# A low-rank step one loop step later, its lines drained by two engines, and zero products issued as pairs of row halves

## The chip, the cores and the metric

The kernel runs on one core of a Trainium2 chip. The time is that of the whole launch on the device, in microseconds (us). The core's engines are TensorE (PE in the profile; PEld are its weight loads), VectorE (DVE), ScalarE (ACT), GpSimd (POOL) and SyncE (SP); each runs its own instructions in order and they meet through semaphores.

## The reference

The input x is 8 batches of 3136 rows and 256 columns, float32. It is first mixed by Fourier transforms, then by a low-rank step over the rows and an MLP over the columns:

```python
X = np.fft.fft(np.fft.fft(x, axis=1), axis=2)
x = X.real
h = x.transpose(0, 2, 1) @ U @ V            # U: 3136 x 32, V: 32 x 3136
u = x + h.transpose(0, 2, 1)
out = u + np.maximum(u @ w_ch1, 0) @ w_ch2  # w_ch1: 256 x 1024, w_ch2: 1024 x 256
```

## The kernel before

The row transform of length 3136 is split as 49 times 64, with the symmetry of real input used so that only 25 of the 49 residues (NK1) are kept. Batches go in four pairs. For every batch there is a table g: for each of the 25 residues 128 rows, of which 64 hold a half-transformed batch and 64 hold the low-rank result te, the same for all 25. One product with the table T then gives both the second half of the transform and the low-rank term; the results go into a tile q, and the MLP reads q.

The front builds the tables (sine values, T, the folded weights) and the g of batch 0. x of batch 0 comes by DMA as the tile X0. x_round issues the products of X0 with the table Fs (quarter_products, line 227; 128 in the first round, 128 in the second), and the results are copied out of PSUM into zt, by copy_act or copy_dve, and from there into g by quarter_rows. line32 (line 204) makes one further row with four products. Ahead of the first round and behind the second PE runs products of zeros (the tile idle, which is a part of W1m) into the PSUM tile that comes next (lines 650 and 674); nobody reads their results. w1_fold (line 679) folds the MLP's first weights. te_single (line 298) computes the low-rank result of one batch from g with 50 products, te_out lets DVE copy it to te, and spread lets POOL write te into the 64 lower rows of g (line 306).

The loop goes over 13 chunks for each pair, with four loop steps each, so 52 steps for each pair (NS). In loop step t of a chunk, mlp1 (line 383, ReLU on ACT in line 385) runs for that chunk, mlp2 (lines 394 and 397) for the chunk before, then what plan has placed at that step, then the outputs are drained (om on ACT in line 406, ob on DVE in lines 407 and 408) and stored by SP (line 412). plan writes the order out by hand: place(steps, lo, hi) spreads a list of steps evenly over the loop steps lo to hi.

For pair 0 the plan holds, among others: turned_steps, which makes the g of batch 1 in loop steps 10 to 17 (products line 227, zt on ACT, eight copies into g on DVE each second step, line 76); te_single of batch 1; the s3_steps of batch 1, twelve groups of four residues and a last one (line 322), each drained from PSUM into q by the engine that is given to it; and the steps of the next pair: loads of x (xa by SP, xb by an indirect DMA of POOL, line 99), folds on POOL (line 144) and DVE (lines 134 to 136), and s1_steps (line 185, drained into z by ACT, line 73). The steps of s1, s3 and te_single share one pool of two PSUM tiles (psd); mlp1 has two of its own (psh), mlp2 has two (pso).

copy_dve is line 76, copy_act line 73. copy_alt calls the two by turns.

Of the kernel before, what the change touches and what calls it, by code (L numbers as in the profile page):

```python
# [22 lines left out]
def kernel(  # L23
# [9 lines left out]
    nc = tc.nc  # L33
# [3 lines left out]
    P = 128  # L37
# [124 lines left out]
    def load_steps(pr):  # L162

        for c in range(8):
            def load(c=c):
                pr.chunks.append(load_pair_chunk(pr.p, c))
            yield load, (lambda c=c: fold_pair_chunk(pr.chunks[c])), (lambda c=c: fold_pair_chunk_d(pr.chunks[c]))
# [92 lines left out]
    def turn(pr, b, parts, engines=(nc.sync,)):  # L260
        g = gpool.tile([P, NK1, D], BF16, tag=f"g{b}", name="g")
        src = zd[pr.p % 2, b].rearrange("k cn d -> cn k d")
        for i, (k0, k1) in enumerate(parts):
            engines[i % len(engines)].dma_start(out=g[0:64, k0:k1], in_=src[:, k0:k1, :])
        pr.g[b] = g

    def te_out(pr, b, ps, c0, s0, spread):
        te = tes[b]
        nc.vector.tensor_copy(te[64:96, 0:129], ps[c0:c0 + 32, 0, 0:129])
        nc.vector.tensor_copy(te[96:128, 129:256], ps[s0:s0 + 32, 0, 129:256])  # L270
        spread(pr.g[b], te)

    def te_steps(pr, spread):

        st = Obj()
        order = [*range(1, 32), 0]

        def step(lo, hi):
            if lo == 0:
                st.ps = psd.tile([P, 2, D], FP32, tag="ps", name="teps")  # L280
            for i in range(lo, hi):
                j = order[i]
                for s, cs in enumerate([slice(0, 129), slice(129, 256)]):
                    nc.tensor.matmul(st.ps[64 * s:64 * s + 64, 0, cs], UZ[:, j, s::2],  # L284
                                     pr.z[:, j, cs], start=(i == 0), stop=(i == 31))
            if hi == 32:
                for b in range(2):
                    te_out(pr, b, st.ps, 32 * b, 64 + 32 * b, spread)

        for lo, hi in [(0, 20), (20, 32)]:  # L290
            yield lambda lo=lo, hi=hi: step(lo, hi)

    def te_single(pr, b, spread, ps=None):

        ps = ps or psd.tile([P, 2, D], FP32, tag="ps", name="teps")
        for k in range(NK1):
            for s, cs in enumerate([slice(0, 129), slice(129, 256)]):
                nc.tensor.matmul(ps[32 * s:32 * s + 32, 0, cs], us[:, k, s::2], pr.g[b][0:64, k, cs],
                                 start=(k == 0), stop=(k == NK1 - 1))
        te_out(pr, b, ps, 0, 32, spread)  # L300

    def spread(parts):
        def run(g, te):
            src = te[64:128].bitcast(I32)
            for eng, k0, k1 in parts:
                eng.tensor_copy(g[64:128, k0:k1].bitcast(I32), src.unsqueeze(1).to_broadcast([64, k1 - k0, D // 2]))  # L306
        return run

    def two(row, a, b, n):

        v = row[:, a:a + n]
        return bass.AP(row.tensor, v.offset, [list(v.ap[0]), [b - a, 2], [1, n]])

    def s3_steps(pr, b, evac):

        if pr.q is None:
            pr.q = qpool[pr.p % 2].tile([P, 2, 6272], BF16, tag="q", name="q")

        def mm(o, k1, blk, st, rows=P, low=None):
            lt = low[:, blk::2] if low is not None else pr.g[b][0:rows, k1, blk::2]  # L320
            r = T[0:rows, k1, 0:64] if k1 == 0 else T[0:rows, k1, :].rearrange("p (s j) -> p s j", s=2)
            nc.tensor.matmul(o, lt, r, start=st, stop=True, skip_group_check=True)  # L322

        def lines(ps, g, blk, rows, low=None):
            for u in range(4):
                us = slice(u * 64, (u + 1) * 64)
                mm(ps[:, 0, us] if 4 * g + u == 0 else ps[:, :, us], 4 * g + u, blk, u == 0 and low is None, rows, low)

        def step(g, blk):
            ps = psd.tile([P, 2, 256], FP32, tag="ps", name="ps")  # L330
            lines(ps, g, blk, P)
            move(ps, g, blk, evac)

        def move_part(ps, g, blk, evac, part):
            lo = 64 if part and g == 0 else 0
            c0 = 3200 + b * 1536 + (4 * g - 1) * 64 if part else b * 1600 + 4 * g * 64
            evac(pr.q[:, blk, c0 + lo:c0 + 256], ps[:, part, lo:256])

        def move(ps, g, blk, evac):
            if g == 0:  # L340
                move_part(ps, g, blk, evac, 0)
                move_part(ps, g, blk, evac, 1)
            else:
                k0 = 4 * g
                evac(two(pr.q[:, blk, :], b * 1600 + k0 * 64, 3200 + b * 1536 + (k0 - 1) * 64, 256), ps[:])

        def last():
            ps = psd.tile([P, 2, 2, 64], FP32, tag="ps", name="ps")
            k1 = NK1 - 1
            for blk in range(2):  # L350
                mm(ps[:, blk], k1, blk, blk == 0)
            for blk in range(2):
                evac(two(pr.q[:, blk, :], b * 1600 + k1 * 64, 3200 + b * 1536 + (k1 - 1) * 64, 64), ps[:, blk])

        yield lines, move_part
        for g in range(6):
            for blk in range(2):
                yield lambda g=g, blk=blk: step(g, blk)
        yield last
# [124 lines left out]
    def bank2(name):  # L484
        return psh.tile([P, 2, 512], FP32, tag="h", name=name)
# [7 lines left out]
    def round_view(ps):  # L493
        return ps.rearrange("p a (i s c k) -> p (a i) s c k", s=2, c=2, k=32)
# [5 lines left out]
    idle = W1m[0][:].rearrange("p a j -> p (a j)")[:, 0:640]  # L500
# [138 lines left out]
    def x_round(ps, i0, n):  # L639
        quarter_products(X0, ps, i0, n)  # L640

        def out(evac):
            j = i0 % 16
            evac(zts[i0 // 16][:, :, :, :, j:j + n].rearrange("p c k s i -> p s c k i"),
                 ps[:, :, :, :, 0:NK1].rearrange("p i s c k -> p s c k i"))
        return out

    tps0 = bank2("tps")
    for i in range(4):
        nc.tensor.matmul(tps0[:, 0], idle[:, 0:P], idle[:, P:640], start=True, stop=True)  # L650
    x_round(round_view(tps0), 0, 8)(copy_act)
    outs = [x_round(round_view(bank_d("tps")), 8 + 4 * i, 4) for i in range(2)]
    z32 = line32(0, bank_o("ps32"))
# [16 lines left out]
    nc.vector.tensor_copy(T[0:64, :, 64:128], T[0:64, :, 63::-1])  # L670

    teps = bank2("teps")
    for i in range(5):
        nc.tensor.matmul(teps[:, 0], idle[:, 0:P], idle[:, P:640], start=True, stop=True)

    def w1_fold(c, banks):
        for blk in range(2):
# [63 lines left out]
    spread_pool = spread([(nc.gpsimd, 0, 9), (nc.gpsimd, 9, 17), (nc.gpsimd, 17, NK1)])  # L741
# [38 lines left out]
    def plan(p):  # L780

        at = [[] for _ in range(NS)]

        def place(steps, lo, hi):
            steps = list(steps)
            for i, s in enumerate(steps):
                at[lo + i * (hi - lo) // len(steps)].append(s)

        def place_next(nx, a, gap, s3lo):

            s1 = list(s1_steps(nx, copy_act))
            for c, (load, fn, fd) in enumerate(load_steps(nx)):
                for o, f in [(0, load), (4, fn), (7, fd), (9, s1[2 * c]), (10, s1[2 * c + 1])]:
                    at[int(a + gap * c) + o].append(f)
            e = int(a + gap * 7) + 11
            place([lambda: (turn(nx, 0, [(0, 8), (8, NK1)]), turn(nx, 1, whole))], e, e + 1)
            place(te_steps(nx, spread_pool), e, e + 2)
            place(list(s3_steps(nx, 0, copy_dve))[1:], s3lo, NS)

        cur = pairs[p]  # L800
        if p == 0:
            rest = []
            for t, f in zip([1, 2, 2, 3, 4, 5, 5, 6, 8], s3b0[4:]):
                at[t].append(f)
            at[0].append(lambda: w2_fold(0))
            at[2].append(lambda: w2_fold(1))
            place([late_tables], 8, 9)
            place([load_uz], 24, 25)
            place([lambda: rest.append(pair_tables())], 6, 7)
            place([lambda: rest[0]()], 10, 11)  # L810
            place(turned_steps(cur, 1, X1), 10, 18)
            place([lambda: te_single(cur, 1, spread_pool)], 18, 19)
            place(list(s3_steps(cur, 1, copy_dve))[1:], 19, 31)
            place_next(pairs[1], 8, 2.6, 44)
        else:
            place(list(s3_steps(cur, 1, copy_dve))[1:], 3, 18)
            if p + 1 < NP:
                place_next(pairs[p + 1], 0, 3.4, 40)
        return at

    for i in range(len(chunks) + 1):
        cur = chunks[i] if i < len(chunks) else None
# [47 lines left out]
```

## Time and profile before

| | |
|---|---|
| median of 5 runs | 452.45 us (451.33 to 455.52) |
| profiled execution | 451.86 us, its span 450.1 us |
| PE busy | 425.7 us, 95% of the span |
| ACT busy | 289.8 us, 64% |
| DVE busy | 225.0 us, 50% |
| POOL busy | 143.0 us, 32% |
| moved by DMA | 64.34 MB, mean 143 GB/s |

All times below are microseconds from the start of the span of the one profiled execution. A group's line names the source line, the engine, the operation, what is written and read, and how often. "x119" counts recorded instructions; some records of matmuls can be missing. A PE time includes the way through the array, so the ends of successive products overlap. In brackets stands the idle time of the engine ahead of the group and what ended it; "issue" means that the profile shows no wait for it.

### The profile page before, as it was taken

How to read it: one execution, taken by the hardware profiler on the slowest of the kernel's cores; microseconds unless marked ns; L12 is line 12 of the kernel's file. 1: busy time of each engine (PE TensorE's matmuls, PEld its weight loads, DVE VectorE, ACT ScalarE, POOL GpSimd, SP SyncE). 2: the span in 40 equal slices, each digit the busy share in tenths (PEclk: the TensorE clock that was granted, in tenths of full speed). 3: DMA queues.
4: the chain of work that ended last, by engine and by line, in shares of the span. 5: the costliest groups of instructions: out<-in, count | busy, mean ns of one | idle time of the engine just before them, and what ended most of it. 6: DMA issues, size and time to landing. Idle time of an engine off the chain costs nothing.

```text
span 450.1 us, 10536 instructions
## 1 busy us (share of the span) xinstructions
PE 425.7 (95%) x4158; PEld 308.0 (68%) x4221; DVE 225.0 (50%) x541; ACT 289.8 (64%) x402; POOL 143.0 (32%) x180
## 2 busy tenths in 40 slices
PE   3789997999999998999999999999999999999995
PEld 1656665777777776767867777776867777667764
DVE  7783686874355367362354367463354344222222
ACT  5786755767565666777565667777466655666662
POOL 7465465941420546350510545550400000000000
PEclk9999999999999999999999999999999999999999
DMA  8649763876683656763772647863662222222323
GB/s 145 160 141 168 205 169 111 254 181 179 171 212 74 170 147 194 234 209 88 161 209 63 170 112 241 225 194 106 162 144 66 71 64 67 72 71 74 80 60 93
DMA packets 59761, 64.34 MB, mean 143 GB/s; under 512 B 12950, under 2 KB 52672, under 8 KB 59552
## 3 DMA queue, kind: packets, MB, share of 16 engines
q1 hardware_dynamic: 50000, 42.68, 36.7%
q0 software_dynamic: 7232, 14.30, 13.5%
q10 hardware_dynamic: 2480, 6.69, 4.0%
q8 instruction: 33, 0.54, 0.5%
q14 instruction: 16, 0.13, 0.1%
HBM read 34.62 MB, written 32.19 MB: 148 GB/s over the span
## 4 chain that ended last, share of the span: by engine, by line
PE 80%; DVE 6%; DMA 5%; issue 3%; SPq 2%; POOL 2%; ACT 1%; DVEq 0%; POOLq 0%
PE ops L394 33%; PE hps L383 32%; PE ps L322 5%; PE ops L397 4%; DMA out_dram<-ob 2%; PE ps L185 2%; DMA X<-in_x_dram 2%; DVE g L76 2%; SPq L412 2%; PE teps L284 1%; PE tps L227 1%; DMA xa<-in_x_dram 1%; DVE q L76 1%; POOL y L144 1%; ACT hT L385 1%
## 5 line engine op out<-in xcount | busy, mean ns | idle before, releaser
L385 ACT ACTIVATE hT<-hps 128x1024 bf16<-128x1024 f32 (+1 forms) x208 | 202.5, 975 | 109.8 <-PE hps L383 103.1
L394 PE MATMUL ops<-W,hT 128*128 128x256 bf16 x1568 | 224.7, 273 | 0.8 <-DVE ob L408 0.6
L394 PEld LDWEIGHTS <-hT 128*128 128x128 bf16 x1568 | 145.1, 98 | 34.9 <-DVE ob L408 0.8
L76 DVE CAST q<-ps 128x512 bf16<-128x512 f32 (+3 forms) x121 | 65.0, 559 | 83.3 <-PE ps L322 81.9
L383 PE MATMUL hps<-q,W1p 128*128 128x512 bf16 (+1 forms) x420 | 103.2, 355 | 2.3 <-DVE q L76 0.5
L407 DVE TENSOR_TENSOR ob<-ops,om 128x256 f32<-128x256 f32 (+1 forms) x102 | 41.8, 409 | 117.7 <-ACT om L406 117.0
L383 PE MATMUL hps<-q,W1m 128*128 128x512 bf16 x351 | 95.7, 379 | 2.1 <-ACT hT L385 0.5
L144 POOL TENSOR_TENSOR y<-xa,xb 98x510 f32<-98x510 f32 (+1 forms) x48 | 61.2, 1295 | 107.3 <-DMA xa<-in_x_dram 102.2
L383 PEld LDWEIGHTS <-W1p 128*128 128x128 bf16 x448 | 40.3, 97 | 26.9 <-issue 1.7
L383 PEld LDWEIGHTS <-W1m 128*128 128x128 bf16 x384 | 35.3, 98 | 26.5 <-issue 1.4
L397 PEld LDWEIGHTS <-q 128*128 128x128 bf16 x392 | 38.4, 98 | 21.2 <-issue 0.6
L406 ACT COPY om<-ops 128x256 f32<-128x256 f32 (+1 forms) x102 | 37.3, 365 | 13.9 <-PE ops L394 7.9
L306 POOL COPY g<-te 64x1024 int32<-64x1024 int32 (+1 forms) x23 | 24.8, 1119 | 57.1 <-DVE te L270 52.5
L408 DVE TENSOR_TENSOR ob<-ops,om 128x256 f32<-128x256 f32 (+1 forms) x102 | 41.0, 402 | 0.0
L73 ACT CAST z<-ps 128x512 bf16<-128x512 f32 x48 | 28.1, 586 | 18.5 <-PE ps L185 18.5
L397 PE MATMUL ops<-Bp,q 128*128 128x128 f16 x200 | 38.4, 219 | 0.0
L322 PE MATMUL ps<-T,g 128*128 128x128 bf16 (+3 forms) x400 | 36.9, 218 | 0.4 <-ACT q L73 0.3
L397 PE MATMUL ops<-Bm,q 128*128 128x128 f16 x192 | 36.9, 219 | 0.0
L322 PEld LDWEIGHTS <-g 128*128 128x128 bf16 (+1 forms) x400 | 29.4, 98 | 5.0 <-POOL g L306 0.4
L99 POOL DMA_INDIRECT xb<-in_x_dram,idx x24 | 24.6, 1023 | 5.4 <-issue 4.5
L135 DVE TENSOR_TENSOR yb<-y 98x508 bf16<-98x508 f32 (+1 forms) x24 | 21.8, 906 | 0.0
L185 PE MATMUL ps<-yb,F 98*128 98x258 bf16 (+1 forms) x108 | 18.9, 265 | 1.7 <-DVE q L76 1.7
(136 smaller groups left out, 205.0 us busy)
## 6 DMA issues: line engine op xcount, KB each, us to landing
out_dram<-ob SPq DMA_DIRECT2D x389, 64.0 KB
xa<-in_x_dram SPq DMA_DIRECT2D x24, 392.0 KB
zturn<-z ACTq DMA_DIRECT2D x9, 512.0 KB
g<-zturn SPq DMA_DIRECT2D x3, 800.0 KB
g<-zturn SPq DMA_DIRECT2D x3, 544.0 KB
X<-in_x_dram POOLq DMA_DIRECT2D x4, 384.0 KB, 7.9
X<-in_x_dram POOLq DMA_DIRECT2D x2, 744.0 KB, 8.0
zturn<-z ACTq DMA_DIRECT2D x3, 448.0 KB
```

Source lines behind the costliest of these rows:

```text
L73: nc.scalar.copy(o, i)
L76: nc.vector.tensor_copy(o, i)
L144: nc.gpsimd.tensor_tensor(ck.y[:, l0:l1, 1:256], ck.xa[:, l0:l1, 1:256], rb[:, l0:l1, 255:0:-1], op=AL.add)
L185: nc.tensor.matmul(o[..., cs], F[:, 2 * t + i].rearrange("p b k c -> p (b k c)"), y[..., cs], start=first, stop=True, skip_group_check=True)
L322: nc.tensor.matmul(o, lt, r, start=st, stop=True, skip_group_check=True)
L383: nc.tensor.matmul(ps[:, i, 0:n], (W1p if ch.sg > 0 else W1m)[jp // 2][:, blk, j], q[:, blk, c0:c0 + n], start=(blk == 0), stop=(blk == 1))
L385: nc.scalar.activation(ch.h[:, 2 * jp:2 * jp + 2, 0:n], ps[:, :, 0:n], AF.Relu)
L394: nc.tensor.matmul(ps, ch.h[:, j, t * P:(t + 1) * P], W2[:, j, :], start=(j == 0 and (t % 2 == 0 or last)), stop=(j == JT - 1), skip_group ...
L397: nc.tensor.matmul(ps[:, j], q[:, j, tk], (Bp if ch.sg > 0 else Bm)[:, j], start=False, stop=False, skip_group_check=True)
L406: nc.scalar.copy(om[:, 0:n], ch.po[:, 0:n, 1])
L407: nc.vector.tensor_tensor(ob[:, 0:n, 0:P], ch.po[:, 0:n, 0], om[:, 0:n], op=AL.add)
L408: nc.vector.tensor_tensor(ob[:, 0:n, P:D], ch.po[:, 0:n, 0], om[:, 0:n], op=AL.subtract)
```

## The change

Two things are changed. In the front, the zero products are issued by a helper, halves, as pairs: each product takes 64 of the 128 rows, the two of a pair write the two banks of the PSUM tile, and their widths are 512 or 256 columns. The four products ahead of the first round become 14, the five behind the second round become 14. In the loop plan of pair 0, te_single of batch 1 is placed in loop step 19 instead of 18, and the s3_steps of batch 1 in 20 to 30 instead of 19 to 30, with copy_alt in the place of copy_dve.

```diff
+    def halves(ps, sizes):
+        for n in sizes:
+            for r in range(2):
+                w = idle[64 * r:64 * r + 64]
+                nc.tensor.matmul(ps[:, r, 0:n], w[:, 0:P], w[:, P:P + n], start=True, stop=True)
+
     tps0 = bank2("tps")
-    for i in range(4):
-        nc.tensor.matmul(tps0[:, 0], idle[:, 0:P], idle[:, P:640], start=True, stop=True)
+    halves(tps0, [512] * 2 + [256] * 5)
     x_round(round_view(tps0), 0, 8)(copy_act)
...
     teps = bank2("teps")
-    for i in range(5):
-        nc.tensor.matmul(teps[:, 0], idle[:, 0:P], idle[:, P:640], start=True, stop=True)
+    halves(teps, [512] * 3 + [256] * 4)
...
             place(turned_steps(cur, 1, X1), 10, 18)
-            place([lambda: te_single(cur, 1, spread_pool)], 18, 19)
-            place(list(s3_steps(cur, 1, copy_dve))[1:], 19, 31)
+            place([lambda: te_single(cur, 1, spread_pool)], 19, 20)
+            place(list(s3_steps(cur, 1, copy_alt))[1:], 20, 31)
             place_next(pairs[1], 8, 2.6, 44)
```

## The prediction

> **What bounds the kernel now.** I read the page first: the span is 450.1 us, and the profiled execution took 451.86 us with what lies around it. TensorE (PE) carries 80% of the chain that ended last, and the granted clock is full throughout.
>
> ```profile
> PE 80%; DVE 6%; DMA 5%; issue 3%; SPq 2%; POOL 2%; ACT 1%; DVEq 0%; POOLq 0%
> q8 instruction: 33, 0.54, 0.5%
> ```
>
> So only PE's stalls are for sale. The second line counts for the front: queue q8 carries 0.54 MB in 33 reads, and PE has 4158 + 4221 recorded instructions; that makes 16 kB and some 255 instructions a read, so these are PE's own instructions, in blocks. The waits of PE then show where it stood:
>
> ```profile
> PE ps L185 <- DVE q L76: 1.7, 2, 1.1
> PE teps L298 <- DVE g L76: 1.7, 2, 1.5
> PE tps L227 <- issue: 1.1, 1, 1.1
> ```
>
> The two places of the change, in the timeline. First the loop (start, length, engine, line, what; in brackets the idle time before, and who ended it):
>
> ```profile
> 68.14 3.04 DVE L76 COPY g<-zt 32x400 bf16<-32x400 bf16 x8 [0.90 <-ACT zt L73]
> ...
> 71.23 1.59 PE L298 MATMUL teps<-g,us 64*32 64x129 bf16 x50 [1.48 <-DVE g L76]
> ...
> 73.97 3.12 POOL L306 COPY g<-te 64x1152 int32<-64x1152 int32 x3 [4.60 <-issue]
> ...
> 75.17 0.57 PE L322 MATMUL ps<-T,g 128*128 128x64 bf16 x8 [0.17 <-POOL g L306]
> 75.58 1.28 DVE L76 CAST q<-ps 128x256 bf16<-128x256 f32 x4 [1.73 <-PE ps L322]
> ...
> 76.33 0.39 PE L185 MATMUL ps<-yb,F 98*128 98x258 bf16 x2 [0.59 <-DVE q L76]
> ```
>
> PE reaches the low-rank step while DVE still writes g and stands 1.48 us. It stands 0.17 us until POOL has spread the result. Then it issues two line products, and the next product L185 wants their PSUM buffer while DVE drains four pieces in a row: 0.59 us. That is 2.24 us, and of 76 to 120 us hardly anything else.
>
> Now the front:
>
> ```profile
> 13.43 1.02 PE L650 MATMUL tps<-W1m 128*128 128x512 bf16 x3 [0.35 <-ACT us L73]
> 15.07 2.16 PE L227 MATMUL tps<-Fs,X 98*32 98x50 f16 x128 [0.61 <-DMA X<-in_x_dram]
> ...
> 18.71 2.03 PE L227 MATMUL tps<-Fs,X 98*32 98x100 f16 x119 [1.14 <-issue]
> ...
> 23.16 0.39 PE L679 MATMUL w1ps<-w_f,Q 128*128 128x512 f32 x1 [0.41 <-issue]
> 23.73 1.59 PE L298 MATMUL teps<-g,us 64*32 64x129 bf16 x50 [0.18 <-DVE g L76]
> ```
>
> The zero products fill the time until x lands at 15.07. Then PE stops after 9 of the 128 products of the second round, for nothing the profile names, until 18.71. From that stop to the next nameless one (23.16) it runs 119 products with their weights (238), 5 zero products (10), four weight loads and three products of L679 (7) and one semaphore instruction: 256. So both stops are PE out of instructions at a block's edge. In the DMA view q8 starts its first read between 16.0 and 16.2 us, its second between 20.8 and 21.0. What those stops cost is told by ACT:
>
> ```profile
> 18.57 0.86 ACT L73 COPY g<-zt 31x800 bf16<-31x800 bf16 x1
> 19.81 1.62 ACT L73 CAST zt<-tps 128x800 bf16<-128x800 f32 x3 [0.38 <-PE tps L227]
> 21.46 2.21 DVE L76 COPY g<-zt 32x800 bf16<-32x800 bf16 x6 [0.56 <-ACT zt L73]
> ```
>
> ACT is in one piece until 19.43, then waits only 0.38 us for PE; DVE and the low-rank product at 23.73 hang on it. So the 1.14 us stop is worth 0.38 us, the 0.41 us one nothing (the product after it waits for DVE anyway).
>
> **The change, the loop part.** The step te_single goes from loop step 18 to 19, so PE runs one more mlp1 (0.86), mlp2 (1.0) and L185 pair (0.22) first. From the end of mlp2 at 69.75 it arrives at about 71.8; DVE's g is there at 71.2. The wait of 1.48 is gone. It ends at 73.4, DVE converts te (two times 0.29) by 74.0, POOL's first spread copy (1.15) ends at 75.2. PE meanwhile has L185, mlp1 and mlp2 (2.1) and arrives at 75.4: the 0.17 is gone by 0.2, a thin cover, and at most 0.3 comes back if POOL is late. POOL's order moves too: the xb load of chunk 4 (0.97 us of POOL) now stands ahead of the spread; POOL idled 4.60 us there, so it is free, and the fold behind the spread starts earlier. The step issues no DMA; SP's order is unchanged. On DVE the g copies and one drain of the outputs stand ahead of te as before.
>
> The drains: s3_steps now alternates. Of the pieces of pair 0, batch 1, ACT takes two of 256, five of 512 and one small one. ACT's price for a 512 piece is that of L73 z<-ps, 586 ns; so ACT gets some 4 us, DVE loses 4.5. At the first group the two engines drain side by side: the buffer is free some 0.4 us after the first product instead of 1.0, so of 0.59 about 0.2 stays. But 13 steps over 11 loop steps instead of 12 put two into loop step 25 as well, with an L185 pair behind them. That pair waits for the first drain: 0.59 to 0.69 of copy less 0.2 of the second step's products, so 0.45 new. After each of the stalls the first two products took 0.39 instead of 0.22 (76.33 against 78.63), so a stall costs 0.17 more than its idle time: three go (2.24 + 0.51), two smaller ones come (0.65 + 0.34). Sum of the loop part: -1.75 us. Bounds: -2.5 (no new stall) to -1.1 (both new ones at the full 0.59 to 0.7 and POOL late).
>
> Does it reach the end? PE is busy 23.84 of 24 us between 96 and 120. The fold of the last chunk ends at 108.98 and PE uses it from 111.24: 2.3 us of slack, enough for 1.75 even if its load does not move. Nothing else is late next.
>
> **The front part.** 4 products of 512 columns become 14 on 64 rows each, 2304 columns a row half; 5 become 14 with 2560. No row of this trace has two row halves at once. Bound below: side by side, like the column tiles of L298 (50 recorded products of 128 columns in 1.59 us, 32 ns each, against 56 ns for the single L322 of 128); then the first fill ends at 14.5, the second lasts 1.1. Bound above: one after the other, 4 x 0.215 + 10 x 0.108 = 1.95 us, to 15.4, 0.35 past the landing; the second 2.15, hidden before L679's weights. I take the lower, nearest to L298, and keep +0.35. The Trainium skill (TensorEngine Tiling: Array Packing, Key Properties) speaks against it: a change of the tiling mode drains the engine. By that rule one drain more would be paid at each fill; no run here prices it.
>
> The larger effect is the 20 instructions more ahead of x. Every block edge comes 20 instructions earlier in the work. The first read now begins about 1.1 us after PE's wait for x ends (16.16 against 15.04); the edge whose passing frees that block lies 256 back from the first stop: 18 for the nine products, 8 for L204, 230 of round one's 256. So it stands 26 instructions into round one, 28 behind the first of the two semaphore instructions of the wait for x. With the change it stands 8 behind. In the steady loop reads start, by my count, 28 to 58 instructions before PE's array reaches the freeing edge (taking the same 1.1 us of latency), and the sequencer's semaphore instructions lie 35 ahead of the array; so the fetch looks up to some 20 beyond the sequencer. 8 is inside that, 28 was not. Then the read is asked for at 13.44 instead of 15.1, arrives by about 15.5, and the stop at 18.71 goes: -0.38. The second edge then falls just before the last product of round two; its read, asked for at 16.8, is usable by about 20, and ACT wants that product at 20.6. Value taken: -0.38; bounds: -0.4 and the rival below. The Trainium skill (Runtime: NRT & Kernel Launch, Instruction fetch mechanics) gives blocks of 256 instructions, which the count above confirms, and says the refill is mostly hidden; here it was not, 1.14 us. By the rule the front part would be worth 0.
>
> **Sum.** 451.86 - 1.75 - 0.38 = 449.7 on the profiled execution's scale. The median of the runs shown is 452.45, 0.59 above it; that gives 450.3 for a median, 2.1 us or 0.47% less. The measurement can tell some 0.5% (2.3 us) from no change, so the forecast sits at that bound.
>
> **Rivals.**
> Fetch not advanced (20%): the fetch does not look 8 ahead of a blocked sequencer. Then the first stop, still until 18.7, hits the fourth product of line 32 (L204), 20 instructions earlier, and the second, still until 23.1, hits the last product of round two (2 + 254 instructions on), which ran before 20.74. ACT's last zt copy moves from about 20.95 to 23.35: +2.4, or +3.0 if the fill pairs run one after the other behind it. With the loop part: +0.65 to +1.25, 453.1 to 453.7 by the median. For it: the 8 is near; against it: the count of the steady loop.
> ACT becomes the bound (12%), the one that ends slower: in a loop step with hT 1.03, z 0.59, q 0.59 and om 0.38 ACT has 2.59 us against PE's 2.25. It decides once ACT is more than one loop step late, because hps has two buffers: then each of seven copies costs PE up to 0.59, 4.1 us, net +2, 454.5. Against it: copies fall on every second step only, and ACT was busy 13.97 of 20 us there; 18 with the copies.
> The stall moves on (6%): the loop gain is lost at the last fold or the UZ load's place on SP, the front gains nothing: 452.
>
> **How the numbers follow.** Forecast 62%: around 450.3 with 0.44 beyond the bound of 0.5% (DVE's relief and the refills are rather underpriced), 0.17 within, 0.01 slower. Fetch rival: 0.02, 0.13, 0.05. ACT: 0.01, 0.04, 0.07. Moved on: 0.01, 0.04, 0.01. Sum: faster 0.48, same 0.38, slower 0.14. Range: from -2.5 - 0.4 with 0.8 of a median's scatter (448.7) to the fetch rival's 453.7.
>
> **What would show it.** Right: no wait of L298 for g near 72 us; the second round of L227 without a nameless stop, q8's first read before 15 us, ACT's zt copies at 19.4; a PE wait of about 0.5 at L185 some 12 us after the step. Wrong: a nameless stop at L204 near 17 us and at L227 near 21; or hps waiting for hT between 76 and 100.

## The result and the profile after

The changed kernel took 453.88 us in the median of 26 runs (451.66 to 460.78), against 453.33 us for the kernel before in 47 runs (450.85 to 456.11). The ratio is 1.0006 [0.999, 1.0023]: no difference that can be told. Forecast were 450.3 us. Repeated on another chip (the last experiment) the ratio was 1.0054 [1.0024, 1.0085]. All ratios leave out executions that took over 1.5% more than the fastest of their kernel, so a ratio is not quite the ratio of the medians.

The profiled execution took 451.94 us with a span of 450.2 us, practically that of before (451.86 and 450.1). The equal spans hide a loss in the front and gains behind it; the waits of PE show where. Page, chain of work that ended last; then the waits of PE (who waited for whom, total us, times, longest):

```profile
PE 86%; DVE 4%; issue 3%; ACT 2%; DMA 2%; SPq 1%; POOL 0%; DVEq 0%; POOLq 0%
```

```profile
PE tps L227 <- issue: 2.7, 1, 2.7
PE ps L204 <- issue: 1.2, 1, 1.2
...
PE ps L185 <- DVE q L76: 0.7, 1, 0.7
PE teps L298 <- DVE g L76: 0.5, 1, 0.5
PE hps L383 <- ACT hT L385: 0.5, 2, 0.2
...
PE ps L185 <- ACT q L73: 0.5, 1, 0.5
```

The 1.5 us wait of L298 for g in the loop is gone, as forecast (the 0.5 that is left is that of batch 0, in the front). But the two nameless stops, 1.14 and 0.41 us before, are now 1.2 and 2.7 us. The front, in the timeline of PE, and below it that of ACT (start, length, what, count, in brackets the idle time before and who ended it):

```profile
13.44 1.15 PE L652 MATMUL tps<-W1m 64*128 64x512 bf16 x14 [0.30 <-ACT us L73]
14.55 2.16 PE L227 MATMUL tps<-Fs,X 98*32 98x50 f16 x128
16.49 0.33 PE L204 MATMUL ps<-x,F 98*32 98x129 bf16 x3
18.00 0.23 PE L204 MATMUL ps<-x,F 98*32 98x127 bf16 x1 [1.18 <-issue]
18.01 2.15 PE L227 MATMUL tps<-Fs,X 98*32 98x100 f16 x127
22.83 0.26 PE L227 MATMUL tps<-Fs,X 98*32 98x100 f16 x1 [2.67 <-issue]
...
25.92 1.59 PE L298 MATMUL teps<-g,us 64*32 64x129 bf16 x50 [0.52 <-DVE g L76]
```

```profile
20.30 1.22 ACT L73 CAST zt<-tps 128x800 bf16<-128x800 f32 x2
23.12 0.49 ACT L73 CAST zt<-tps 128x400 bf16<-128x400 f32 x1 [1.60 <-PE tps L227]
```

PE stops ahead of the fourth product of L204, and again 128 products later ahead of the very last product of round two. That is the rival "fetch not advanced", to the instruction: both blocks of PE's instructions end 20 instructions earlier in the work, and the next ones arrive hardly earlier than before (the stops ended at 18.71 and 23.16, and now at 18.00, with x half a microsecond earlier, and at 22.83). The second stop before cost nothing; now one product of 128 is cut off by it, ACT's last zt piece hangs on that product, and all of batch 0 on ACT. The low-rank step of batch 0 starts at 25.92 instead of 23.73.

The loop, from the step on: timelines of PE, ACT and DVE.

```profile
74.35 1.59 PE L298 MATMUL teps<-g,us 64*32 64x129 bf16 x50
...
77.99 0.57 PE L322 MATMUL ps<-T,g 128*128 128x64 bf16 x8
79.22 0.38 PE L185 MATMUL ps<-yb,F 98*128 98x258 bf16 x2 [0.66 <-DVE q L76]
...
91.53 0.38 PE L185 MATMUL ps<-yb,F 98*128 98x258 bf16 x2 [0.45 <-ACT q L73]
```

```profile
77.17 1.02 ACT L385 ACTIVATE hT<-hps 128x1024 bf16<-128x1024 f32 x1
78.40 0.65 ACT L73 CAST q<-ps 128x256 bf16<-128x256 f32 x2 [0.21 <-PE ps L322]
```

```profile
78.80 0.63 DVE L76 CAST q<-ps 128x192 bf16<-128x192 f32 x2 [0.85 <-ACT q L73]
```

No bracket ahead of L298 and L322: 1.48 and 0.17 us are gone. The 0.45 us wait at the loop step with two s3 steps, 12.3 us later, came at exactly its forecast size. The wait ahead of L185 stayed (0.66, before 0.59): the two engines do not drain side by side there. ACT begins at 78.40, as soon as a product is there; DVE begins only at 78.80, and the profile has it waiting for ACT's q (inferred by the profile; no run tests why).

To see where the two kernels stand to each other, I took three points at which PE waits for the same thing in both (the weights W1p; hT near 123 and near 425). A fourth point, a product of mlp2 near 64 us, lies between the front and the changed steps of the loop. Timeline of PE, kernel before, then the changed one:

```profile
29.51 1.02 PE L383 MATMUL hps<-q,W1p 128*128 128x512 bf16 x4 [0.44 <-DVE W1p L447]
63.22 0.27 PE L394 MATMUL ops<-W,hT 128*128 128x256 bf16 x1 [0.28 <-DVE ob L408]
122.73 1.94 PE L383 MATMUL hps<-q,W1m 128*128 128x512 bf16 x8 [0.25 <-ACT hT L385]
424.80 1.94 PE L383 MATMUL hps<-q,W1m 128*128 128x512 bf16 x8 [0.25 <-ACT hT L385]
```

```profile
31.70 1.02 PE L383 MATMUL hps<-q,W1p 128*128 128x512 bf16 x4 [0.44 <-DVE W1p L447]
65.82 0.27 PE L394 MATMUL ops<-W,hT 128*128 128x256 bf16 x1 [0.67 <-DVE ob L408]
124.24 1.02 PE L383 MATMUL hps<-q,W1m 128*128 128x512 bf16 x4 [0.25 <-ACT hT L385]
424.88 1.94 PE L383 MATMUL hps<-q,W1m 128*128 128x512 bf16 x8 [0.25 <-ACT hT L385]
```

The changed kernel is 2.19 us behind after the front, 2.60 near 64 us, 1.51 after the loop of pair 0, and 0.08 at the end. The step near 64 us is the wait for ob, which stands ahead of the changed steps and varies from profile to profile (none in e4 and e8, 0.15 to 0.79 us in the others). From there to the wait for hT near 123 us the kernel before takes 59.51 us and the changed one 58.42: the changed loop steps gain 1.09 us here, not the forecast 1.75. Of the 1.43 us between the last two points 1.09 is one stall of the kernel before at 174.4 (L185 waits for DVE's q) that this execution of the changed kernel does not have; the other 0.34 is not accounted for. The stall hangs on where POOL's fold happens to fall. Timeline of DVE and POOL, before, then after:

```profile
171.30 1.75 DVE L135 TENSOR_TENSOR yb<-y 98x508 bf16<-98x508 f32 x1
...
171.15 3.03 POOL L144 TENSOR_TENSOR y<-xa,xb 98x510 f32<-98x510 f32 x2 [4.63 <-DMA xa<-in_x_dram]
```

```profile
172.81 0.68 DVE L135 TENSOR_TENSOR yb<-y 98x508 bf16<-98x508 f32 x1
...
174.11 2.48 POOL L144 TENSOR_TENSOR y<-xa,xb 98x510 f32<-98x510 f32 x2 [4.66 <-DMA xb<-in_x_dram,idx]
```

Beside POOL's fold DVE's yb took 1.75 us, alone 0.68. Such a stall came in four of the later profiles too (e1, e6, e8 and e10, at 174 to 280 us) and not in six others (e2, e3, e4, e5, e7 and e9), with both loop plans among those that have it and among those that don't. So I take it as scatter, and the ends of two profiles can't be set against each other; the loop part has to be sized by timed runs and by the stretch from 64 to 123 us.

### The profile page after: what moved, and what is told of

The parts are those of the page before. It is cut to its first block, busy times and chain, and to the rows that moved or that the text cites. A ratio compares the mean times of both kernels' runs of the same rounds, so it can differ in the third digit from the quotient of the medians.

```text
span 450.2 us, 10579 instructions
## 1 busy us (share of the span) xinstructions
PE 426.2 (95%) x4180; PEld 308.9 (69%) x4240; DVE 224.5 (50%) x533; ACT 294.2 (65%) x410; POOL 144.0 (32%) x180
## 4 chain that ended last, share of the span: by engine, by line
PE 86%; DVE 4%; issue 3%; ACT 2%; DMA 2%; SPq 1%; POOL 0%; DVEq 0%; POOLq 0%
PE ops L394 35%; PE hps L383 35%; PE ps L322 5%; PE ops L397 4%; PE ps L185 3%; DMA out_dram<-ob 2%; PE tps L227 2%; PE teps L284 1%; SPq L412 1%; ACT hT L385 1%; DVE g L76 1%; PE teps L298 1%; DVE ob L408 0%; DVE ta L447 0%; DVE q L76 0%
## 5 line engine op out<-in xcount | busy, mean ns | idle before, releaser
L76 DVE CAST q<-ps 128x512 bf16<-128x512 f32 (+3 forms) x113 | 60.9, 559 | 84.1 <-PE ps L322 80.9
L144 POOL TENSOR_TENSOR y<-xa,xb 98x510 f32<-98x510 f32 (+1 forms) x48 | 62.8, 1329 | 103.5 <-DMA xa<-in_x_dram 88.6
L322 PE MATMUL ps<-T,g 128*128 128x128 bf16 (+3 forms) x400 | 36.8, 218 | 0.3 <-ACT q L73 0.3
L322 PEld LDWEIGHTS <-g 128*128 128x128 bf16 (+1 forms) x400 | 29.3, 98 | 4.6 <-DVE q L76 0.4
L135 DVE TENSOR_TENSOR yb<-y 98x508 bf16<-98x508 f32 (+1 forms) x24 | 24.5, 1020 | 0.0
L76 DVE COPY g<-zt 32x400 bf16<-32x400 bf16 (+3 forms) x45 | 17.2, 382 | 9.4 <-ACT zt L73 8.8
```

The source lines that it names most:

```text
L76: nc.vector.tensor_copy(o, i)
L144: nc.gpsimd.tensor_tensor(ck.y[:, l0:l1, 1:256], ck.xa[:, l0:l1, 1:256], rb[:, l0:l1, 255:0:-1], op=AL.add)
```

## Experiments

Two theories to begin with. "Fetch": the front loses some 2.2 us because the fetch does not run ahead of PE's sequencer while that waits for x, and the loop part wins what was forecast. Rival "tiles": the row halves themselves, as another way of tiling, cost the front its time. A second question was which edit of the loop earns what. Ratios are to the kernel before on the same chip, with 95% intervals.

**e1: the loop part alone** (the front of before):

```diff
-            place([lambda: te_single(cur, 1, spread_pool)], 18, 19)
-            place(list(s3_steps(cur, 1, copy_dve))[1:], 19, 31)
+            place([lambda: te_single(cur, 1, spread_pool)], 19, 20)
+            place(list(s3_steps(cur, 1, copy_alt))[1:], 20, 31)
```

> The front of the kernel before, the loop plan of the change. Theory (the front costs, the loop gains): the front's numbers return (first nameless stop of PE inside round two until about 18.7 us, low-rank product of batch 0 at 23.7), no PE wait of 1.48 us ahead of the low-rank step of batch 1, a new PE wait of about 0.45 at L185 where two line steps share a loop step; time 1.0 to 1.8 us below the kernel before, ratio 0.996 to 0.998. Rival (the loop part is worth nothing on its own, because the stall only moves to the double step and to the drains): ratio 0.999 to 1.001, the sum of PE's idle time in the loop as before.

Measured: 450.61 us against 451.68, ratio 0.9959 [0.9934, 0.9985], which is -1.85 us (-0.7 to -3.0); the medians lie 1.07 apart. In its profile the waits of 1.48 and 0.17 us are gone, and 0.66 and 0.45 stand at L185, as in the changed kernel. From the product of mlp2 at 63.00 to the wait for hT at 121.41 it takes 58.41 us, 1.10 less than before (58.41 in e3 and 58.40 in e10, too). So the loop part gains; the times put it between 0.7 and 3.0 us, PE's timeline at 1.1.

**e2: the front part alone** (the loop plan of before):

```diff
-            place([lambda: te_single(cur, 1, spread_pool)], 19, 20)
-            place(list(s3_steps(cur, 1, copy_alt))[1:], 20, 31)
+            place([lambda: te_single(cur, 1, spread_pool)], 18, 19)
+            place(list(s3_steps(cur, 1, copy_dve))[1:], 19, 31)
```

> The front of the change, the loop plan before. Theory (the 20 instructions more put the block edges at L204's fourth product and at the last product of round two): nameless stops at these two places again, the low-rank product of batch 0 near 25.9 us instead of 23.7, and all behind it 2.2 us later; time 2.2 us above the kernel before, ratio 1.004 to 1.006. Rival (the late front is made up again by later waits, the loop gave nothing): ratio 0.999 to 1.002.

Measured: 456.14 us against 451.68, ratio 1.0085 [1.0047, 1.0123]. The front part makes it slower, by more than the 2.2 us of the stops and more than the 1.004 to 1.006 expected. Timeline of PE, and the table of stretches (stretch, us, busy time and count of PE, PEld, DVE, ACT and POOL, granted clock, DMA share, GB/s):

```profile
18.73 0.23 PE L204 MATMUL ps<-x,F 98*32 98x127 bf16 x1 [1.73 <-issue]
...
23.00 0.30 PE L227 MATMUL tps<-Fs,X 98*32 98x100 f16 x1 [1.38 <-issue]
```

```profile
17.00:20.00 3.00, 1.27 (x67) 1.27 (x70) 2.79 (x8) 1.14 (x4) 0.42 (x2) 0.85 0.79 209
20.00:25.00 5.00, 3.62 (x88) 2.34 (x81) 1.60 (x6) 3.81 (x7) 1.06 (x3) 0.50 0.67 146
...
30.00:35.00 5.00, 5.00 (x44) 4.30 (x38) 1.42 (x4) 1.24 (x4) 3.78 (x3) 0.50 0.00 0
35.00:40.00 5.00, 4.55 (x27) 2.13 (x27) 3.75 (x6) 3.04 (x4) 4.28 (x10) 0.89 0.38 51
```

The stops sit at the same two products; the low-rank product of batch 0 came at 27.48, not near 25.9. In this execution something came on top that the prediction had no term for: after the first stop the granted clock falls to half and stays there until about 36 us. That is not so in every execution. A stretch of 8 us at half clock lowers the mean clock of a 450 us span to 0.991, and I counted the executions at or below that. On this chip it was 0 of 34 of the kernel before and 0 of 12 of e1, but 7 of 11 of e2. Their median was 458.89, that of e2's other four 453.81: 2.1 us above before, which is the front's 2.2.

**e3: six more products ahead of x**, 12 instructions with their weight loads, so that the block's edge comes 4 instructions ahead of PE's wait for x:

```diff
-    halves(tps0, [512] * 2 + [256] * 5)
+    halves(tps0, [512] * 2 + [256] * 2 + [128] * 6)
```

> As the changed kernel, with the first fill as ten pairs instead of seven over the same 2304 columns: 12 instructions more ahead of x, so that the freeing edge of the first block stands 4 instructions ahead of the wait for x instead of 8 behind it. Theory (the fetch is asked for when the sequencer passes the edge, and a sequencer that waits for x does not pass it): the first read of q8 starts 1.1 us after the fill begins at 13.4, near 14.5 or when x is through, instead of 15.5; the stop of 1.2 us at L204 goes; the second stop falls some 14 instructions before the end of round two and ends by 20.5 instead of 22.8; low-rank product of batch 0 at 23.0 to 23.8, time 2 to 3 us below the changed kernel, ratio to the kernel before 0.995 to 0.998. Rival (the read begins only when x is through the DMA engines, or the fetch is not tied to the edge): first read again near 15.5, both stops stay, time as the changed kernel.

Measured: 453.81 us, ratio 1.0043 [1.0012, 1.0075]. Timeline of PE:

```profile
17.41 0.27 PE L227 MATMUL tps<-Fs,X 98*32 98x100 f16 x3 [0.79 <-issue]
...
22.88 0.33 PE L227 MATMUL tps<-Fs,X 98*32 98x100 f16 x7 [3.12 <-issue]
```

The places moved by six products, as they should: the last seven products of round two are now cut off. But the first read of q8 started at 15.03 and not near 14.5, the second stop lasted until 22.88 and not 20.5, and the ratio is far from 0.995 to 0.998; that expectation was missed. In this execution x was early: PE's sequencer had passed its wait for x by 14.0 us. The read followed 1.0 us after that, as in the kernel before and the changed one, so an edge that lies ahead of the wait bought nothing. Why is open: x's own packets were on the way until 14.72, and no run tells whether they held the read. The second read started at 20.49, as in the changed kernel, although its edge was passed earlier, and that asked for another cause (e9).

**e4: as many instructions, on all 128 rows**, one after the other in one bank (fill issues one product on all rows for each width):

```diff
-    halves(tps0, [512] * 2 + [256] * 5)
+    fill(tps0, [256] * 4 + [128] * 10)
...
-    halves(teps, [512] * 3 + [256] * 4)
+    fill(teps, [256] * 6 + [128] * 8)
```

> As the changed kernel, but each fill as 14 products on all 128 rows instead of 7 pairs of row halves; the same number of instructions, 2304 and 2560 columns in all. Theory (only the number of instructions counts, not the row halves): nameless stops at L204's fourth product and at the last product of round two as in the changed kernel, ratio to the kernel before 0.999 to 1.002. Rival (the pairs of row halves themselves cost, by what a change of the shape does on PE): the stops move or the fill ends earlier and the low-rank product of batch 0 comes over 0.5 us earlier than 25.9.

Measured: 453.64 us, ratio 1.0043 [1.0011, 1.0074]. Timeline of PE:

```profile
13.43 1.15 PE L650 MATMUL tps<-W1m 128*128 128x256 bf16 x14 [0.35 <-ACT us L73]
...
19.28 0.23 PE L204 MATMUL ps<-x,F 98*32 98x127 bf16 x1 [1.73 <-issue]
...
23.28 0.26 PE L227 MATMUL tps<-Fs,X 98*32 98x100 f16 x1 [1.84 <-issue]
```

The same two products stop with no row half anywhere: the number of instructions decides where PE stops, and "tiles" falls. The ratio is above the 0.999 to 1.002 expected; 4 of its 10 executions had a mean clock at or below 0.991, the profiled one among them.

**e8: only the second fill changed** (the first as before, the loop plan of the change). The first edge then lies where it lay before, and the second must fall into the fill itself:

```diff
     for i in range(4):
         nc.tensor.matmul(tps0[:, 0], idle[:, 0:P], idle[:, P:640], start=True, stop=True)
...
-    for i in range(5):
-        nc.tensor.matmul(teps[:, 0], idle[:, 0:P], idle[:, P:640], start=True, stop=True)
+    halves(teps, [512] * 3 + [256] * 4)
```

> The loop plan of the change, the first fill of the kernel before (4 products on 128 rows), the second fill of the change (7 pairs). Theory (the instructions ahead of x move both edges; those behind round two only what follows): the first stop is inside round two as in the kernel before, with 9 products of it done; the second edge falls into the second fill, 18 instructions on, so PE stops there until 22.8 to 23.2, then low-rank product of batch 0 at 24.2 to 24.8, against 23.3 with the front of before and 25.9 with that of the change; ratio to the kernel before 0.998 to 1.001. Rival (the late front is the pairs' own cost or the second fill's): stops at L204 and at the last product of round two, low-rank product at 25.5 or later.

Measured: 452.94 us against 452.9, ratio 0.9993 [0.9963, 1.0023]. Timeline of PE:

```profile
18.84 2.03 PE L227 MATMUL tps<-Fs,X 98*32 98x100 f16 x119 [1.25 <-issue]
20.81 1.04 PE L652 MATMUL teps<-W1m 64*128 64x512 bf16 x9
23.12 0.50 PE L652 MATMUL teps<-W1m 64*128 64x256 bf16 x5 [1.28 <-issue]
```

Exactly 9 of the 14 products run ahead of the second stop: 119 and 9 products with their weight loads are 256 instructions. The count holds to the instruction, and L298 began at 24.68, between before (23.73) and the change (25.92).

**e9: the load of the first folded weights later**, behind a gate of POOL that the second half's load already has. It was executed once, since its own new wait spoils the time:

```diff
-    w1_f = [load_w1(0)]
-
...
     nc.gpsimd.tensor_copy(gate[32:33, 1:2], g0[32:33, 0, 64:65])
+    w1_f = [load_w1(0)]
     w1_f.append(load_w1(1))
```

> The changed kernel with the first load of w_ch1 (512 KB) issued behind POOL's gate at about 20.4 us instead of at 16.6, so that fewer bytes are under way when PE's second block of instructions is asked for; the same instructions in the same order on PE. Theory (the second read is asked for when the first stop ends, and is then held by the loads under way, which end at 20.2 to 20.5 in every run so far): the second read of q8 starts 1.0 to 1.5 us after the first stop's end, near 19.2 instead of 20.4, and the second stop ends near 21.6 instead of 22.8; w1_fold then waits for its late weights, so the low-rank product of batch 0 comes no earlier than 26 and the time says nothing. Rival (the second read follows the first by a fixed interval, or the loads do not matter): read again at 20.4 to 20.9, stop to 22.8.

Measured: 459.37 us in one run. Timeline of PE:

```profile
17.53 0.23 PE L204 MATMUL ps<-x,F 98*32 98x127 bf16 x1 [0.35 <-issue]
...
20.98 0.26 PE L227 MATMUL tps<-Fs,X 98*32 98x100 f16 x1 [1.31 <-issue]
...
25.17 1.96 PE L682 MATMUL w1ps<-w_f,Q 128*128 128x512 f32 x4 [2.74 <-DMA w_f<-in_moe_w_ch_dram]
```

Without that load under way the second read of q8 started at 18.65 instead of 20.43, and the second stop ended at 20.98 instead of 22.83. Part of this is that x was earlier here and the first stop ended at 17.53 instead of 18.00. Counted from that end, the read started after 1.12 us instead of 2.43, and the second stop took 1.31 us instead of 2.67. So PE's instruction read stands behind data loads: this load makes half of the second stop, 1.36 us. In the other eleven profiles the read started at 20.4 to 21.8, within 0.9 us of the load's last packet (20.7 to 21.5); e3 and e5, whose first stops ended as early as here (17.41 and 17.69), are among them. It is one execution.

**e5, e6, e7: the loop part taken apart** (front of before): the move alone (with copy_dve), the second engine alone (steps 18 and 19 to 30), and the whole with one s3 step less crowded:

```diff
# e5
+            place([lambda: te_single(cur, 1, spread_pool)], 19, 20)
+            place(list(s3_steps(cur, 1, copy_dve))[1:], 20, 31)
# e6
+            place([lambda: te_single(cur, 1, spread_pool)], 18, 19)
+            place(list(s3_steps(cur, 1, copy_alt))[1:], 19, 31)
# e7
+            place([lambda: te_single(cur, 1, spread_pool)], 19, 20)
+            place(list(s3_steps(cur, 1, copy_alt))[1:], 20, 32)
```

> The front of the kernel before; te_single in loop step 19, the line steps in 20 to 30, all drained by DVE as before. Theory (the move alone brings the gain, by closing the 1.48 us wait; the second drain engine adds little, since its share waited for the first engine's): PE's wait at L185 behind the first two line steps 0.6 to 0.7 us as with two engines, the one in the double step 0.5 to 0.6, time 0.2 us within that of the loop part with both, ratio to the kernel before 0.995 to 0.998. Rival (DVE's relief carries it): ratio 0.999 to 1.001, more PE waits at L185 for DVE between 76 and 110 us than with two engines.

> The front of the kernel before, te_single in loop step 18 and the line steps in 19 to 30 as before, drained by two engines. Theory (drains are not what PE waits for): the waits of 1.48 and 0.17 us stay, the 0.59 at L185 stays within 0.1, ratio 0.998 to 1.001. Rival (ACT's copies make hps wait): PE waits for hT of ACT between 76 and 100 us, ratio above 1.002; or a gain by DVE's relief, ratio below 0.998.

> The front of the kernel before, the loop plan of the change with the line steps spread over 20 to 31 instead of 20 to 30, so that only loop step 20 holds two of them. Theory (the new wait of 0.45 us at L185 belongs to the double step 25): it goes, and with it some 0.65 us; time 0.4 to 0.8 us below the loop part as it is, ratio to the kernel before 0.994 to 0.996. Rival (the wait belongs to ACT's drain and not to the double step): a wait of about 0.45 us at L185 stays at some step.

Measured, against 452.9 us: e5 452.51, ratio 0.9981 [0.9953, 1.0009]; e6 452.95, 0.9998 [0.9969, 1.0028]; e7 450.88, 0.9957 [0.9927, 0.9987]. Waits of PE in e6, and the one at L185 in the timeline of e7:

```profile
PE ps L185 <- DVE q L76: 1.7, 2, 1.1
PE teps L298 <- DVE g L76: 1.5, 1, 1.5
```

```profile
77.81 0.38 PE L185 MATMUL ps<-yb,F 98*128 98x258 bf16 x2 [0.66 <-DVE q L76]
```

The second engine alone removes no wait: 1.48 ahead of L298, 0.17 and 0.66 are still there in e6. In e7 the wait at the double step is gone and of these waits the 0.66 is all that is left. e5's waits at L185 are nearly those of the change, with DVE in the place of ACT at the double step (0.59 and 0.56), and two nameless stops of 0.23 and 0.52 us at 82 and 87 us come on top. By the times, how the gain splits between the move and the second engine can't be told: the intervals of e5, e6 and the whole overlap. PE's timeline, one profile each, says the move: from the product of mlp2 near 64 us to the wait for hT near 123 us it is 59.51 us before, 59.75 in e6, 59.31 in e5 with its nameless stops (58.56 without), 58.41 in e1 and 57.82 in e7. e7 has the lowest ratio of all, but is not told apart from e1 either (0.9957 and 0.9959, on two chips).

**e10: the changed kernel once more**, no edit, on another chip:

> The changed kernel once more, to be set beside its parts. Theory (the parts add: loop part 0.996, front part 1.0085 with wide intervals, and part of the front's price is a half clock that follows the long stop in a share of the executions): ratio 1.000 to 1.005, executions above 455 us have a mean granted clock under 0.992, and stops at L204 and at the last product of round two in the profile. Rival (the parts help each other: with the late front the loop's waits fall away by phase): ratio 0.998 to 1.000.

Measured: 455.66 us against 452.74, ratio 1.0054 [1.0024, 1.0085]. Timeline of PE:

```profile
20.66 0.23 PE L204 MATMUL ps<-x,F 98*32 98x127 bf16 x1 [2.70 <-issue]
...
24.11 0.30 PE L227 MATMUL tps<-Fs,X 98*32 98x100 f16 x1 [0.70 <-issue]
```

Here x came at 15.68, a microsecond late, the first read of q8 fell among the loads and started only at 17.96, and it was the first stop that took 2.70 us. The sum of the stops is much the same (3.4 and 3.85 us); 6 of 8 executions had the clock at or below 0.991. The parts, e1's -0.41% and e2's +0.85%, add up to +0.44%: the two measurements of the change, +0.06% and +0.54%, lie on either side of it.

## Why the prediction was wrong

**The step that failed** is "so the fetch looks up to some 20 beyond the sequencer", and with it "8 is inside that" and the term of -0.38 for the front. It came from counting in the steady loop, where the position of the sequencer against the array was itself an estimate. The read was to be asked for at 13.44, while PE stood at its wait for x. In no profile did it start before that wait had ended. It started 1.04 to 1.20 us after the end in eight of the twelve, whether the edge lies 28 instructions behind the wait (before), 8 behind (the change) or 4 ahead of it (e3); in e2, e7 and e8 it was 1.6 to 1.7 us, in e10 2.4. So in the changed kernel it started at 15.52 for a wait that ended at 14.44, took about 1 us, and PE went on 1.5 us after its end. From the end of the wait until PE went on, 3.75 us passed before and 3.56 after. The front cost +2.19 us by the profile, +2.1 by the executions of e2 with a mean clock above 0.991, where -0.38 was forecast. The rival had priced it at +2.4, and its two stops stood where it said. That the edges move with the number of instructions is shown (e2, e4, e8); why the fetch does not start earlier is not, since in e3 it did not either, though there the edge lies ahead of the wait.

**A term was missing.** I asked what the stops cost in time, not what they do to the clock. In the profiles of e2, e3, e4 and e10 PE ran at half clock for some 7 to 17 us afterwards. Counted by a mean clock at or below 0.991, this befell 7 of 11 executions of e2, 4 of 12 of e3 and 4 of 10 of e4, where before and e1 had none in 46 on that chip; by the medians such executions took 3.3 to 5.1 us longer than the others of their kernel. The length of a stop alone does not decide: the clock fell after a stop of 1.73 us (e2) and did not fall after one of 2.67 us (the changed kernel's profile). The clock records of the traces show a pattern behind this. Apart from the last microseconds of each span, the stretches at half clock last 3.41, 6.83, 10.24 and 17.07 us, which are 1, 2, 3 and 5 times 3.41. Cut each span into intervals of 3.41 us, counted from a change of its clock: seven times in the twelve profiles the clock fell before the end of the work, each time at the end of an interval in which PE had stood idle for 1.49 to 2.74 us. The largest idle time in an interval without a fall behind it was 1.53 us. The stop of 2.67 us lay across a border at 21.60, with 1.44 us on one side and 1.23 on the other. So where a stop falls counts beside its length. By TensorE: Matmul & The Clock Gate, Part 1, of the Trainium skill, the gate goes to half after an idle window of about 3.4 us. The length agrees with the 3.41 us here; PE need not be idle for the whole of it, since 1.49 to 2.74 us were enough.

On another chip the kernel before had a mean clock at or below 0.991 in 6 of 35 executions by itself. On the chip of the first measurement its clocks are not listed (the changed kernel's are: 10 of 29), but 17 of its 47 times lie at 454.3 us or above, where the executions with a low clock lie elsewhere; that may be why the ratio there is 1.0006 and not the 1.0044 of the parts. It was not shown.

**The second read** was forecast to be "asked for at 16.8" and "usable by about 20". The edge that frees its block lies 256 instructions back from the second stop, and that is the first stop itself, which lasted until 18.00. The read then started 2.43 us later, of which the load of w_ch1 makes some 1.3 (e9), and the stop lasted until 22.83. The rival had it right by taking the old time, 23.1, and not by knowing why.

**The loop term**, -1.75, has the right sign, and its waits came as forecast but for one: the 1.48 and the 0.17 went (0.20 us of the latter stand in e8's profile, where POOL was late, as the bounds allowed), the 0.45 came. "At the first group the two engines drain side by side", with about 0.2 of 0.59 left, was wrong: 0.66 stayed, as DVE began 0.40 us behind ACT. That is some 0.46 us too much gain. The 0.17 us more that each stall was to cost does not show either: the waits at these places fell from 2.24 to 1.11 us, by 1.13, and PE's timeline from 64 to 123 us is shorter by 1.09 (the change) to 1.11 (e10). That is the lower bound given, -1.1. The ratio of e1, -1.85 with -0.7 to -3.0, allows both sizes. "ACT becomes the bound" did not happen: PE's waits for hT are 0.5 us as before. "The stall moves on" did not either; the fold of the last chunk had its slack.

**The fill itself** was right: 14 row halves took 1.15 us, as long as 14 products on all rows with half as many columns in sum (e4), so they do run side by side. x was there when the fill ended (14.55, with no wait ahead of the products), and no drain at the change of tiling showed (0.30 us of idle ahead of the fill, 0.35 before, both put down to ACT; none behind it). This weighed nothing beside the instruction count.

**The refill.** The blocks of 256 instructions that the Trainium skill (Runtime: NRT & Kernel Launch, Instruction fetch mechanics) gives hold to the instruction here (e8). The prediction's division was slightly off: (4158 + 4221) / 33 is 254, not 255. The same section says that a refill is mostly hidden. In the front it is not: the first stop took 0.35 to 2.70 us in the twelve profiles, the second 0.41 to 3.12 in eleven, and only in e1 does none show, where PE waited for the folded weights instead. PE runs 256 instructions, 128 small products and their weight loads, in 2.2 us; from the end of the wait for x until PE went on behind the first stop it took 3.3 to 4.1 us in eleven profiles and 5.1 in e10.

## What to carry to other kernels

Count PE's instructions, not only their time: where a stretch issues 256 of them in less than a refill takes, the block edge is a stall with a fixed place in the program, and any instruction added ahead of it moves that stall onto another product, so ask who waits for that product. A fill that keeps PE busy should be made of few, wide products. And a trace's nameless stop ("issue") that costs nothing today is a price to be kept in mind: it becomes a cost as soon as an edit shifts it.

## What the runs showed of the hardware

- PE's instruction reads (queue q8, 16 kB) share the DMA engines with data: the same read started at 18.65 without the 512 kB load of w_ch1 under way, at 20.4 to 21.8 us with it.
- Stops of PE of 1.73 to 3.12 us were followed by half clock for 7 to 17 us, and one of 2.67 us was not; the clock fell some 0.3 to 1.5 us after the stop's end (e2, e3, e4, e10). Apart from the end of the span, stretches at half clock are multiples of 3.41 us, and the clock fell at the end of 3.41 us intervals with 1.49 to 2.74 us of idle time. The loop's wait for g, which the change removes, did it too: 1.49 us in e2, then half clock for 3.41 us from 80.5.
- Products of 64 rows on the two row halves, in two PSUM banks, ran side by side: 14 of them, 2304 columns a half, in 1.15 us; 14 on all rows with 2304 columns in sum took 1.15 us too (e4).
- DVE's yb (L135) took 1.75 us beside POOL's fold and 0.68 without it.
